# LayerNorm, 32-head attention and a mish gate on one core: b1 loaded as 14 rows, x tiles 1 and 3 on a second DMA queue, one tile's statistics on ScalarE, and a lead-in ordered by other planner numbers

## The chip, the cores and the metric

The kernel runs on one core of a Trainium2 chip. Its engines run programs of their own and wait for each other through semaphores: TensorE (PE, with its weight loads shown as PEld), VectorE (DVE), ScalarE (ACT), GpSimd (POOL) and SyncE (SP), which here does nothing but start DMA transfers. Other engines can start transfers too, on queues of their own.

The metric is the device time of one execution in microseconds. It is the median of several runs. One more execution was recorded by the hardware profiler; all durations below are from that one.

## The reference

All arrays are float32: x is 2048x512, wq and wo 512x512, wk and wv 512x16, w1 512x1792, b1 1792, w2 1792x512. The work is a LayerNorm without gain, attention with 32 query heads of width 16 over one shared key and value head, and a dense layer with mish whose result gates the attention's.

```python
xn = _layernorm(x, axis=-1)
# attention
q = (xn @ wq).reshape(B, S, 32, 16).transpose(0, 2, 1, 3)
k = xn @ wk
v = xn @ wv
p = softmax(einsum("bhqd,bkd->bhqk", q, k) * 16 ** -0.5)
o = einsum("bhqk,bkd->bhqd", p, v)
s = o.transpose(0, 2, 1, 3).reshape(B, S, 512) @ wo
# gate
h = xn @ w1 + b1
act = h * tanh(softplus(h))
g = silu(act @ w2)
return x + s * g
```

## The kernel before

**The tiling.** The 2048 rows of x are 16 tiles of 128 rows, in four chunks of four. To keep float32 precision on TensorE, a matrix is split into a high and a low part (type fp32r), and a product is three matmuls (high by high, high by low, low by high). So weights are loaded raw (`rawwq`, `rawws`, `rawwb`), the high part is copied by ACT (L467) and the low part subtracted on POOL (L169). There is one raw buffer of each kind, so that a load on SP's queue waits until POOL has split the one before it.

**The steady state.** Once the kernel is under way, each step of about 2.9 us on PE does, for the attention, scores twice: `m` (L1069) with the keys as columns, from which DVE takes row maxima (`mb`, L1073, 0.6 us each), and `e` (L1041), from which ACT makes the exponentials (`pts`, L1046); it sums the values (`pv`, L1127); and it fills PE's rest with matmuls of the dense layers (`xps`, L116). Those groups end in an eviction by ACT (`hb` with the bias `b1c`, L785), and mish runs as a chain of small jobs on ACT and POOL: Exp (`t`, L791), three operations on POOL (`t`, `u`, `u`), a product on POOL (`hb`), then Ln and Exp on ACT (`t`, L800 and L804), and another product on POOL.

**The lead-in.** The first 80 us have no such steps yet. There x is loaded and normalized, transposed on PE (`xp`, L298), multiplied with wq (`xps`, L112), wk and wv (`kp`, L339); the q rows go through small DMAs into the tiles `qt` (L741, twelve for each head, from `qh` and `ql`), and the key tile `ks` is written by ACT (high part, L344) and by DVE or POOL (low part), after which a DMA copies it to the other half of the partitions (`k_move`, L355; chunks 1 to 3 as two moves). As soon as q and a chunk of keys are there, the m matmuls of head 0 run, then those of head 1, each two halves: in the names, `m_0_24` is half 0 of block 24, whose keys are in chunk 3 (blocks 0 to 7 use chunk 0, and so on; blocks 4 to 7 of each eight use the later q DMAs). `qt_77` is head 0 and `qt_78` head 1. When head 0 has all 64 maxima, `c_rows` (L1092 to L1112) reduces them and sends them by eight DMAs into `qt_77`, after which the first wave of steps starts (first `xps` at L116).

**What sets the order.** The program is written by a list scheduler in Python. Each operation of the lead-in is a `task` on an engine with a planned duration, dependencies, an earliest time and a priority (L1302 to L1366); a loop takes what can start first, issues it, and advances that engine's planned time. Where PE has nothing ready, it emits three matmuls of a dense group (`fill(3)`) or a matmul without use that keeps PE's clock up (`keep_warm`, L1380, tile `warm`). The instructions of each engine then run on the chip in just this order, whatever the true durations are. So numbers in this planner move instructions on all engines. `xat` is the planned arrival time of an x tile; the tasks of the norm are `norm_a` (`ve`), `norm_b` (`rstd`, two ACT operations) and `norm_c` (DVE, first chunk) or `norm_d` (six small POOL operations, other chunks). The statistics of tiles 0 to 11 are `bn_stats` and `bn_aggr` on DVE (L239, L240), those of tiles 12 to 15 two accumulating passes on ACT (L244, L248).

**The bias.** `b1c` holds b1 as 128 rows by 14 columns, column t for hidden units 128 t to 128 t + 127. It is loaded by one DMA on SP's queue (L1288) that gathers single floats. Its only readers are the `hb` evictions (L785).

Of the kernel before, what the change touches and what calls it, by code (L numbers as in the profile page):

```python
# [14 lines left out]
F32 = mybir.dt.float32  # L15
F32R = mybir.dt.float32r
AF = mybir.ActivationFunctionType
# [3 lines left out]
P = 128  # L21
S = 2048
D = 512
# [7 lines left out]
NFT = F // P  # L31
# [91 lines left out]
def block_kernel(ctx: ExitStack, tc: tile.TileContext, x, wq, wk, wv, wo, w1, b1, w2, out):  # L123
    nc = tc.nc
    cp = ctx.enter_context(tc.tile_pool(name="const", bufs=1))
    sb = ctx.enter_context(tc.tile_pool(name="work", bufs=2))
    ps_e = ctx.enter_context(tc.tile_pool(name="ps_e", bufs=3, space=bass.MemoryType.PSUM))
    ps_m = ctx.enter_context(tc.tile_pool(name="ps_m", bufs=3, space=bass.MemoryType.PSUM))
    ps_v = ctx.enter_context(tc.tile_pool(name="ps_v", bufs=1, space=bass.MemoryType.PSUM))
# [4 lines left out]
    pe, act, dve, pool, sp = nc.tensor, nc.scalar, nc.vector, nc.gpsimd, nc.sync  # L134
# [51 lines left out]
    ident = cp.tile([P, P], F32, name="ident")  # L186
# [15 lines left out]
    b1c = cp.tile([P, NFT], F32, name="b1c")  # L202
# [4 lines left out]
    xr = x.rearrange("o (t p) d -> (o t) p d", p=P)  # L207
# [11 lines left out]
    xin = {}  # L219

    def load_x(c):
        for tt in range(4):
            if 4 * c + tt < NPT:
                xin[c, tt] = pts[:, 4 * c + tt]
            else:
                xin[c, tt] = sb.tile([P, D], F32, tag=("y0", "sc")[tt % 2], name=f"xin{c}_{tt}", bufs=1)
            sp.dma_start(xin[c, tt], xr[4 * c + tt])
            if (c, tt) == (1, 0):
                sp.dma_start(wkv[:, 0], wk.rearrange("(t p) n -> p t n", p=P))
                sp.dma_start(wkv[:, 1], wv.rearrange("(t p) n -> p t n", p=P))  # L230
                wk_split()

    mvs = cp.tile([P, NKT, 2], F32, name="mvs")

    nms = cp.tile([P, 4], F32, name="nms")

    def stats(t):
        st = sb.tile([P, 6], F32, tag="st", name=f"st{t}")
        dve.bn_stats(st, xin[divmod(t, 4)])  # L239
        dve.bn_aggr(mvs[:, t], st)  # L240

    def stats_sum(t):
        w = sb.tile([P, D], F32, tag="u", name=f"sq{t}", bufs=2)
# [80 lines left out]
    vp_of = {}  # L324
# [38 lines left out]

    def v_transpose(c):
        if c == 0:
            vp = vp_of[c] = ps_v.tile([P, 4, 32], F32, tag="v", name=f"vp{c}")
            for tt in range(4):
                pe.transpose(vp[:, tt], vt_of[c][0:32, P * tt:P * (tt + 1)], ident[0:32, 0:32])
        else:
            vp = vp_of[c] = ps_v.tile([P, 2, 2, HALF], F32, tag="v", name=f"vp{c}")  # L370
            for j in range(2):
                pe.transpose(vp[:, j], vt_of[c][:, P * j:P * (j + 1)], ident)

    def v_out(c):
        if c == 0:
            dve.tensor_copy(vaug[:, 0:4, 0:DH], vp_of[c][:, :, 16:32])
        else:
            act.activation(vaug[:, 4 * c:4 * c + 4, 0:DH].rearrange("p (h j) n -> p h j n", h=2),
                           vp_of[c][:, :, :, 48:64].rearrange("p j h n -> p h j n"), AF.Copy)
# [867 lines left out]
    def task(eng, us, fn, deps=(), **kw):  # L1247
        t = Task(eng, us, fn, deps, **kw)
        plan[eng].append(t)
        return t  # L1250
# [28 lines left out]

    step[0] = (0.0 - E0) / STEP_US  # L1280
    new_xt("w")
    xat = {0: 3.4, 1: 3.8, 2: 4.6, 3: 5.3}
    dma_t[0], T["SP"] = 6.4, 2.0
    load("wq")
    load_x(1)
    xat.update({t: landed(DMA_US) for t in range(4, 8)})
    load("ws")
    sp.dma_start(b1c, b1.rearrange("(t p) -> p t", p=P))  # L1288
    load_x(2)
    load_x(3)  # L1290
    xat.update({t: landed(DMA_US) for t in range(8, 16)})
# [11 lines left out]
        b.append([t, *users])  # L1303

    st = [task("DVE", 0.83, lambda t=t: stats(t), at=xat[t], prio=t // 4 * 2) for t in range(12)]
    for t in range(12, 16):
        ss = task("ACT", 0.8, lambda t=t: stats_sum(t), at=xat[t], prio=4)
        st.append(task("ACT", 0.8, lambda t=t: stats_var(t), [ss], prio=4))
    kv_done = None
    for c in range(NC):  # L1310
        z = slice(4 * c, 4 * c + 4)
        ne, eng = (("POOL", pool), ("DVE", dve))[c == 0]
        na = task(ne, 0.2, lambda z=z, eng=eng: norm_a(z, eng), st[z])
        nb = task("ACT", 0.45, lambda z=z: norm_b(z), [na], prio=c and 1)
        nrm = task(ne, 0.8 if c == 0 else 1.0, lambda z=z, n=(norm_d, norm_c)[c == 0]: n(z), [nb])
        xs = []
        for t in range(4 * c, 4 * c + 4):
            e, us = ("ACT", 0.8) if t % 2 or c == 3 else ("DVE", 0.55) if c == 0 else ("POOL", 0.8)
            sc = task(e, us, lambda t=t: x_scale(t), [nrm], prio=c and 1)
            tr = task("PE", 0.6, lambda t=t: x_transpose(t), [sc], fill=c > 0)  # L1320
            if c == 0:
                hi = task("ACT", 0.5, lambda t=t: x_high(t), [tr])
                lo = task("DVE", 0.62, lambda t=t: x_low(t), [hi], lat=-0.9 if t == 3 else 0.1)
            else:
                lo = task("ACT", 0.62, lambda t=t: x_copy(t), [tr], prio=1)
            if t != 3:
                bank("e", 3, tr, [lo])
            xs.append(lo)
        if c == 0:
            st[4].deps.append(nrm)  # L1330
            for k in st[5:12]:
                k.deps.append(xs[-1])

            def q_first():
                xt_done[0] = step[0]
                fill(12)
            xs = [task("PE", 2.8, q_first, xs)]
        else:
            for k in range(2):
                def keep_x(c=c, k=k):  # L1340
                    xt_keep(c, k)
                    landed(KEEP_US / 2)
                task("SP", 0.5, keep_x, xs, prio=2)
        kus = 0.5 if c else 0.7
        k0 = kp = task("PE", kus, lambda c=c: k_proj(c, (0,)), xs)
        for dt in range(1, 4):
            kp = task("PE", kus, lambda c=c, dt=dt: k_proj(c, (dt,)), [kp], lat=0.0)
        kv_done = kp
        kh = task("ACT", 0.76 if c else 0.59, lambda c=c: k_high(c), [kp])
        def low(c=c):  # L1350
            k_low(c)
            if c == 0:
                kready[0] = now[0] + 0.85, 1e9
        vc = task("ACT", 0.4 if c else 0.59, lambda c=c: v_copy(c), [kp])
        kl = task("POOL", 1.4, low, [kh, vc]) if 0 < c < 3 else task("DVE", 0.86 if c else 0.68, low, [kh])
        if c == 0:
            for t in plan["ACT"]:
                if t.prio == 4:
                    t.deps.append(kh)

        def mv(c=c):
            k_move(c)
            kready[c] = (kready[0][0] if c == 0 else now[0] + 3.1, now[0] + (3.1 if c else 2.6))
        moved = task("SP", 1.0 if c else 0.5, mv, [kl])
        if c == 0:
            lead["moved"] = moved  # L1366
        if c == 0:
            vc.deps = [kl]
        bank("v", 1, k0, [kh, vc] if 0 < c < 3 else [kl, vc])
        vtr = task("PE", 0.5, lambda c=c: v_transpose(c), [vc], fill=c > 0)  # L1370
        vo = task("ACT" if c else "DVE", 0.24, lambda c=c: v_out(c), [vtr])
        bank("v", 1, vtr, [vo])

# [302 lines left out]
```

## Time and profile before

| | |
|---|---|
| median of 3 runs | 1568.08 us (1567.94 to 1568.29) |
| the profiled execution | 1567.96 us |
| its span, first to last instruction | 1566.2 us |
| granted TensorE clock | 1.00 of full speed |
| PE busy | 1554.0 us, 99% of the span |
| DVE busy | 1348.7 us, 86% |
| ACT busy | 1290.5 us, 82% |
| POOL busy | 635.7 us, 41% |
| first m matmul of head 0 | 22.07 us after the span's start |
| first matmul of the first wave (L116) | 79.73 us |

Times in the views are microseconds from the start of the span, and the profiled execution is 1.8 us longer than its span. A row of the timeline gives start, duration, engine, line of the kernel, operation, output and inputs, shapes, and how many instructions are drawn together; in square brackets stands how long the engine was idle before it, and what ended that. "SPq" is SP's queue of DMA starts, whose rows are the time that SP took to start the transfer, not the transfer. "issue" is idle time that no release seen in the profile explains. A row of a chain of waits gives start, duration and what the end was waiting for then.

### The profile page before, as it was taken

The numbers are of one execution on the slowest core, as the hardware profiler recorded it, in microseconds if no ns is written. First come the engines' busy times: TensorE is split into PE (matmuls) and PEld (weight loads), VectorE is DVE, ScalarE is ACT, GpSimd is POOL, SyncE is SP. The second block draws the span as 40 slices with busy tenths as digits, with TensorE's granted clock in tenths as the row PEclk, the third lists the DMA queues.
The fourth block names the chain that finished last, engine by engine and source line by source line (L and its number), as shares of the span: only waits on it lengthen the run. The fifth ranks groups of instructions, "written<-read, shape, count | busy, mean of one in ns | idle before, by whom it ended". The sixth has DMA issues, their size and how long they took to land.

```text
span 1566.2 us, 31403 instructions
## 1 busy us (share of the span) xinstructions
PE 1554.0 (99%) x11723; PEld 873.7 (56%) x11723; DVE 1348.7 (86%) x2281; ACT 1290.5 (82%) x2501; POOL 635.7 (41%) x668
## 2 busy tenths in 40 slices
PE   9999999999999999999999999999999999999998
PEld 5555655655555565565555556556555555655644
DVE  7988888888988988888898988888889998888844
ACT  6488888789898778977989788897788978888796
POOL 5787449356356202431625422163152323314122
PEclk9999999999999999999999999999999999999999
DMA  7243134133151303203113320322321213031110
GB/s 220 75 138 119 46 100 150 29 112 112 42 160 50 108 16 112 72 20 104 52 56 112 92 92 17 104 67 76 105 59 41 97 56 111 24 99 32 34 63 28
DMA packets 73863, 125.47 MB, mean 80 GB/s; under 512 B 21536, under 2 KB 35136, under 8 KB 73712
## 3 DMA queue, kind: packets, MB, share of 16 engines
q1 hardware_dynamic: 73568, 123.21, 25.4%
q8 instruction: 93, 1.52, 0.4%
q14 instruction: 58, 0.48, 0.1%
q10 hardware_dynamic: 144, 0.26, 0.0%
HBM read 75.57 MB, written 26.21 MB: 65 GB/s over the span
## 4 chain that ended last, share of the span: by engine, by line
PE 96%; DVE 1%; ACT 1%; DMA 1%; issue 0%; POOL 0%; SPq 0%; POOLq 0%
PE xps L116 43%; PE pv L1127 32%; PE m L1069 12%; PE e L1041 7%; PE xps L112 1%; DVE mb L1073 1%; PE wop L116 1%; PE kp L339 0%; DMA pts<-in_dram 0%; DVE st L239 0%; DMA qt<-ql 0%; DMA rawwb<-in_dram 0%; ACT pts L1046 0%; PE y2ps L116 0%; PE wop L112 0%
## 5 line engine op out<-in xcount | busy, mean ns | idle before, releaser
L1073 DVE TENSOR_REDUCE mb<-m 128x1 f32<-128x512 f32 x2048 | 1266.7, 683 | 169.2 <-PE m L1069 136.0
L1046 ACT ACTIVATE pts<-e 128x512 f32<-128x512 f32 x2048 | 1066.2, 607 | 219.8 <-PE e L1041 153.9
L1069 PE MATMUL m<-ks,qt 48*128 48x512 f32 (+1 forms) x2048 | 842.5, 425 | 0.9 <-DVE mb L1073 0.5
L1041 PE MATMUL e<-qt,ks 64*128 64x512 f32 x2048 | 749.4, 407 | 0.4 <-ACT pts L1046 0.4
L1127 PE MATMUL pv<-pts,vaug 128*32 128x512 f32 x4096 | 532.8, 603 | 0.0
L1069 PEld LDWEIGHTS m<-ks,qt 48*128 48x128 f32 (+1 forms) x2048 | 367.8, 185 | 106.1 <-DVE mb L1073 52.4
L1041 PEld LDWEIGHTS e<-qt,ks 64*128 64x128 f32 x2048 | 372.8, 186 | 29.2 <-ACT pts L1046 23.2
L116 PE MATMUL xps<-wbs,act 64*128 64x512 f32 x1248 | 315.3, 397 | 0.0
L116 PE MATMUL xps<-xt,ws 64*128 64x512 f32 x1128 | 313.2, 410 | 0.4 <-ACT pts L1046 0.3
L116 PEld LDWEIGHTS xps<-xt,ws 64*128 64x128 f32 x1128 | 194.4, 185 | 183.3 <-ACT pts L1046 121.4
L116 PEld LDWEIGHTS xps<-wbs,act 64*128 64x128 f32 x1248 | 226.2, 185 | 65.7 <-ACT pts L1046 32.7
L1127 PEld LDWEIGHTS pv<-pts,vaug 128*32 128x32 f32 x4096 | 87.4, 108 | 150.6 <-issue 142.1
L169 POOL TENSOR_TENSOR hb<-hb,t 128x512 f32<-128x512 f32 x56 | 72.3, 1291 | 168.7 <-ACT t L804 88.4
L179 POOL TENSOR_SCALAR t<-t 128x512 f32<-128x512 f32 x56 | 34.4, 614 | 174.6 <-ACT t L791 174.4
L116 PE MATMUL xps<-xt,wq 64*128 64x512 f32 x336 | 93.0, 409 | 0.0
L116 PEld LDWEIGHTS xps<-xt,wq 64*128 64x128 f32 x336 | 57.9, 185 | 55.2 <-ACT pts L1046 37.7
L169 POOL TENSOR_TENSOR oc<-oc,sc 128x512 f32<-128x512 f32 (+1 forms) x16 | 20.6, 1287 | 153.1 <-DMA wbs<-w 39.8
L116 PE MATMUL xps<-wbs,ot_all 64*128 64x512 f32 x288 | 79.3, 407 | 0.0
L116 PEld LDWEIGHTS xps<-wbs,ot_all 64*128 64x128 f32 x288 | 49.5, 184 | 46.9 <-ACT pts L1046 28.5
L169 POOL TENSOR_TENSOR act<-hb,act 128x512 fp32r<-128x512 f32 x56 | 72.2, 1289 | 4.7
L169 POOL TENSOR_TENSOR hb<-hb,u 128x512 f32<-128x512 f32 x56 | 72.2, 1290 | 4.4
L169 POOL TENSOR_TENSOR u<-u,t 128x512 f32<-128x512 f32 x56 | 71.9, 1285 | 4.7
(151 smaller groups left out, 884.9 us busy)
## 6 DMA issues: line engine op xcount, KB each, us to landing
wbs<-w SPq DMA_DIRECT2D x38, 512.0 KB
ws<-w SPq DMA_DIRECT2D x36, 512.0 KB
qt<-qh SPq DMA_DIRECT2D x256, 32.0 KB
w<-wbs SPq DMA_DIRECT2D x14, 512.0 KB
wq<-wq SPq DMA_DIRECT2D x14, 512.0 KB
wbs<-wo SPq DMA_DIRECT2D x12, 512.0 KB
rawws<-in_dram SPq DMA_DIRECT2D x20, 256.0 KB
w<-ws SPq DMA_DIRECT2D x10, 512.0 KB
```

Of the source, the lines that this page charges most:

```text
L112: self.pe.matmul(ps, self.lhs(), self.rhs(), start=(self.k == 0), stop=(self.k == self.tot - 1))
L116: i = self.pe.matmul(ps, self.lhs()[o], self.rhs()[o], start=(self.k == 0 and self.halves == 0), stop=(self.k == self.tot - 1 and self.hal ...
L169: eng.tensor_tensor(out=o, in0=a, in1=b, op=op)
L179: pool.tensor_scalar(o, o, lim, 0.0, op0=ALU.min, op1=ALU.max)
L1041: pe.matmul(e, ks[o:o + 64, P * k:P * (k + 1)], q[o:o + 64, p], start=True, stop=True)
L1046: x = act.activation(dst, e, AF.Exp, scale=0.25)
L1069: pe.matmul(m, q[o, p, P * t:P * (t + 1)], ks[o, C * kb:C * (kb + 1)], start=True, stop=True)
L1073: return dve.reduce_max(out=mb_of[v][:, kb, z:z + 1], in_=m, axis=AX.X)
L1127: pe.matmul(o[32 * j:32 * j + 32], vaug[:, k], pt, start=(k == 0), stop=(k == 15))
```

## The change

It has four parts.

1. Tiles 1 and 3 of the first chunk of x are started by ACT on its own DMA queue; SP starts tiles 0 and 2, and all the rest as before.
2. b1 is loaded as 14 rows of 128 consecutive floats (`b1r`). PE transposes it into the same PSUM tile as the first chunk's values (`vp`), and ACT copies it from there into `b1c`. The DVE copy of the values into `vaug` reads the same tile and stands ahead of it.
3. The statistics of tile 1 are made on ACT by `stats_one`: two passes over the tile and two copies of single columns.
4. Three planner numbers: the arrivals of x tiles 0 and 1, the duration of `norm_d`, and that of the new statistics task.

```diff
@@ load_x
-            sp.dma_start(xin[c, tt], xr[4 * c + tt])
+            (act if c == 0 and tt % 2 else sp).dma_start(xin[c, tt], xr[4 * c + tt])
...
+    b1r = cp.tile([NFT, P], F32, name="b1r")
...
+    ms1 = cp.tile([P, 2], F32, name="ms1")
+
+    def stats_one():
+        x_ = xin[0, 1]
+        w = [sb.tile([P, D], F32, tag=g, name=f"s1{g}", bufs=2) for g in "ut"]
+        act.activation(w[0], x_, AF.Identity, scale=-1.0 / 8192, accum_out=ms1[:, 0:1])
+        act.activation(w[1], x_, AF.Square, scale=1.0 / 16, bias=ms1[:, 0:1], accum_out=ms1[:, 1:2])
+        act.activation(mvs[:, 1, 0:1], ms1[:, 0:1], AF.Copy, scale=-16.0)
+        act.activation(mvs[:, 1, 1:2], ms1[:, 1:2], AF.Copy, scale=0.5)
...
@@ v_transpose, c == 0
-            vp = vp_of[c] = ps_v.tile([P, 4, 32], F32, tag="v", name=f"vp{c}")
+            v_b1 = ps_v.tile([P, P + NFT], F32, tag="v", name=f"vp{c}")
+            vp = vp_of[c] = v_b1[:, 0:P].rearrange("p (t n) -> p t n", n=32)
+            vp_of["b1"] = v_b1[:, P:P + NFT]
+            pe.transpose(vp_of["b1"], b1r, ident[0:NFT, 0:NFT])
...
@@ v_out, c == 0
             dve.tensor_copy(vaug[:, 0:4, 0:DH], vp_of[c][:, :, 16:32])
+            act.activation(b1c, vp_of["b1"], AF.Copy)
...
-    xat = {0: 3.4, 1: 3.8, 2: 4.6, 3: 5.3}
+    xat = {0: 4.3, 1: 4.3, 2: 4.6, 3: 5.3}
...
-    sp.dma_start(b1c, b1.rearrange("(t p) -> p t", p=P))
+    sp.dma_start(b1r, b1.rearrange("(t p) -> t p", p=P))
...
+    plan["DVE"].remove(st[1])
+    st[1] = task("ACT", 2.2, stats_one, at=xat[1])
...
-        nrm = task(ne, 0.8 if c == 0 else 1.0, lambda z=z, n=(norm_d, norm_c)[c == 0]: n(z), [nb])
+        nrm = task(ne, 0.8 if c == 0 else 1.8, lambda z=z, n=(norm_d, norm_c)[c == 0]: n(z), [nb])
```

The planner then writes the lead-in in another order on every engine. From the first matmul of the first wave on, PE's program is the same as before. PE's `warm` matmuls at L1380 go from 14 to 5. Line numbers of the changed kernel are larger by 11 to 15 behind the new functions (L1069 becomes L1084). The three places that the prediction speaks of follow.

The first place is PE between the projection of k and v of chunk 0 (`kp`) and the first m matmuls. Before:

```order
L339 MATMUL kp_268<-xt_173,wk_90 64x512 x12
L1380 MATMUL warm<-qt_79 128x512
L298 MATMUL xp_312<-ident,pts 128x128 x4
L1380 MATMUL warm<-qt_79 128x512
L298 MATMUL xp_323<-ident,pts 128x128 x4
L1380 MATMUL warm<-qt_79 128x512
L298 MATMUL xp_334<-ident,pts 128x128 x4
L1069 MATMUL m_0_0_343<-ks,qt_77 128x512
```

Now:

```order
L350 MATMUL kp_273<-xt_175,wk_90 64x512 x12
L112 MATMUL xps<-xt_175,xtw 128x512 x6
L309 MATMUL xp_326<-ident,pts 128x128 x4
L1084 MATMUL m_0_0_335<-ks,qt_77 128x512
L1084 MATMUL m_0_1_340<-ks,qt_77 128x512
L1084 MATMUL m_0_2_350<-ks,qt_77 128x512
L380 MATMUL vp_353<-ident,b1r 128x14
L382 MATMUL vp_353<-ident,vt_338 128x32 x4
```

The three warm matmuls are gone, six matmuls of a dense group (`xps` from the first w1 tile `xtw`) stand ahead of the first transposes of chunk 1, and only one x tile of that chunk is transposed ahead of the first m.

On ACT at the same place, the new copy of the bias stands among the norm's operations. Now (there was no such row before):

```order
L355 ACTIVATE ks<-kp_273 48x512
L211 ACTIVATE pts<-pts,nbias,rstd 128x512 x2
L371 ACTIVATE vt_338<-kp_273 32x512
L327 ACTIVATE xf_0_346<-xp_326 128x2x128
L327 ACTIVATE xf_1_347<-xp_326 128x2x128
L272 ACTIVATE rstd<-ve 128x4
L273 ACTIVATE rstd<-rstd 128x4
L391 ACTIVATE b1c<-vp_353 128x14
L255 ACTIVATE sq_366,nms<-pts 128x512
```

The high part of the keys (`ks`) now comes ahead of both x tiles' scaling instead of between them. `b1c` must follow the DVE copy `vaug`, which on DVE stands behind the first four maxima.

The second place is SP's queue around the move of key chunk 3 (the last `ks<-ks`, two transfers). Before:

```order
L355 DMA ks<-ks 48x256 x2
L514 DMA rawws_654<-in_dram 128x4x128
L516 DMA rawwb_675<-in_dram 128x512
L966 DMA xtk_677<-xf_0_616 128x1024
L966 DMA xtk_677<-xf_1_617 128x1024
L514 DMA rawws_701<-in_dram 128x4x128
L516 DMA rawwb_715<-in_dram 128x512
L355 DMA ks<-ks 48x256 x2
L514 DMA rawws_809<-in_dram 128x4x128
L514 DMA rawws_887<-in_dram 128x4x128
```

Now:

```order
L366 DMA ks<-ks 48x256 x2
L529 DMA rawws_674<-in_dram 128x4x128
L531 DMA rawwb_695<-in_dram 128x512
L981 DMA xtk_699<-xf_0_636 128x1024
L981 DMA xtk_699<-xf_1_637 128x1024
L529 DMA rawws_762<-in_dram 128x4x128
L531 DMA rawwb_774<-in_dram 128x512
L366 DMA ks<-ks 48x256 x2
L529 DMA rawws_882<-in_dram 128x4x128
L1127 DMA qt_77<-cr_912 2x8x32 x8
```

The rows read alike, but the loads ahead of the last move are the next pair of weights: one pair more has been loaded further up. A load waits for POOL's split of the tile before it (`xtw` and `wbs`), and these splits now stand behind the first mish chain. On POOL, before:

```order
L169 TENSOR_TENSOR xtw<-rawws_654,xtw 128x512
L169 TENSOR_TENSOR wbs<-rawwb_675,wbs 128x512
L179 TENSOR_SCALAR t_0_738<-t_0_738 128x512
L794 TENSOR_SCALAR u_0_739<-t_0_738 128x512
L169 TENSOR_TENSOR u_0_739<-u_0_739,t_0_738 128x512
L169 TENSOR_TENSOR hb_0_730<-hb_0_730,u_0_739 128x512
L169 TENSOR_TENSOR xtw<-rawws_701,xtw 128x512
```

and now:

```order
L169 TENSOR_TENSOR xtw<-rawws_583,xtw 128x512
L169 TENSOR_TENSOR wbs<-rawwb_598,wbs 128x512
L179 TENSOR_SCALAR t_0_704<-t_0_704 128x512
L809 TENSOR_SCALAR u_0_705<-t_0_704 128x512
L169 TENSOR_TENSOR u_0_705<-u_0_705,t_0_704 128x512
L169 TENSOR_TENSOR hb_0_697<-hb_0_697,u_0_705 128x512
L169 TENSOR_TENSOR xtw<-rawws_674,xtw 128x512
L169 TENSOR_TENSOR wbs<-rawwb_695,wbs 128x512
```

So the load `rawwb_774`, and behind it the key move, wait for the split of `rawwb_695`, four mish operations later than the split of `rawwb_675` that they waited for.

The third place is the start of the first wave. PE before, from the last group ahead of it:

```order
L1069 MATMUL m_1_9_969<-ks,qt_78 128x512
L112 MATMUL xps<-xt_173,ws_844 128x512 x6
L1069 MATMUL m_0_10_983<-ks,qt_78 128x512
L1069 MATMUL m_1_10_986<-ks,qt_78 128x512
L1069 MATMUL m_0_11_991<-ks,qt_78 128x512
L1069 MATMUL m_1_11_994<-ks,qt_78 128x512
L116 MATMUL xps<-xt_173,ws_913 128x512
L1069 MATMUL m_1_12_999<-ks,qt_78 128x512
```

and now:

```order
L1084 MATMUL m_1_9_967<-ks,qt_78 128x512
L112 MATMUL xps<-xt_175,ws_833 128x512 x6
L1084 MATMUL m_0_10_983<-ks,qt_78 128x512
L1084 MATMUL m_1_10_986<-ks,qt_78 128x512
L1084 MATMUL m_0_11_989<-ks,qt_78 128x512
L1084 MATMUL m_1_11_992<-ks,qt_78 128x512
L112 MATMUL xps<-xt_175,ws_833 128x512 x3
L116 MATMUL xps<-xt_175,ws_921 128x512
L1084 MATMUL m_1_12_1007<-ks,qt_78 128x512
```

The last three matmuls of the dense group now stand behind the four m matmuls, so that nothing lies between that group's end and the wave that wants its PSUM bank.

On ACT at this place, before:

```order
L800 ACTIVATE t_1_796<-u_1_797,two 128x512
L785 ACTIVATE hb_4_981<-xps,b1c 128x512
L1046 ACTIVATE pts<-e_0_0_1_1003 128x512
L1046 ACTIVATE pts<-e_0_1_1_1011 128x512
L1046 ACTIVATE pts<-e_1_0_1_1019 128x512
L1046 ACTIVATE pts<-e_1_1_1_1025 128x512
L804 ACTIVATE t_1_796<-t_1_796 128x512
L1046 ACTIVATE pts<-e_0_0_0_1045 128x512
L1046 ACTIVATE pts<-e_0_1_0_1053 128x512
L1046 ACTIVATE pts<-e_1_0_0_1061 128x512
L1046 ACTIVATE pts<-e_1_1_0_1067 128x512
L800 ACTIVATE t_2_919<-u_2_920,two 128x512
```

and now:

```order
L815 ACTIVATE t_1_801<-u_1_802,two 128x512
L819 ACTIVATE t_1_801<-t_1_801 128x512
L815 ACTIVATE t_2_895<-u_2_896,two 128x512
L819 ACTIVATE t_2_895<-t_2_895 128x512
L800 ACTIVATE hb_4_1003<-xps,b1c 128x512
L1061 ACTIVATE pts<-e_0_0_1_1011 128x512
L1061 ACTIVATE pts<-e_0_1_1_1019 128x512
L1061 ACTIVATE pts<-e_1_0_1_1027 128x512
L1061 ACTIVATE pts<-e_1_1_1_1033 128x512
L1061 ACTIVATE pts<-e_0_0_0_1052 128x512
L1061 ACTIVATE pts<-e_0_1_0_1060 128x512
L1061 ACTIVATE pts<-e_1_0_0_1068 128x512
```

Three mish operations (`t_1` at L804, `t_2` at L800 and L804, the latter just behind the last row shown of before) have moved from between the first exponentials to ahead of them.

## The prediction

> **What bounds the kernel now.** I read the page first: busy time by engine, and the chain of work that ended last.
>
> ```profile
> PE 1554.0 (99%) x11723; PEld 873.7 (56%) x11723; DVE 1348.7 (86%) x2281; ACT 1290.5 (82%) x2501; POOL 635.7 (41%) x668
> PE 96%; DVE 1%; ACT 1%; DMA 1%; issue 0%; POOL 0%; SPq 0%; POOLq 0%
> ```
>
> PE is the bound nearly everywhere, and behind the lead-in its program does not change. So the change can only move the time at which PE settles into its steady pace, and every microsecond of that goes one for one into the end. Next I asked for busy time by stretch around the first wave, for the sums over DVE in the lead-in, and for the longest pieces of the chain of waits.
>
> ```profile
> 70.00:80.00 10.00, 9.43 (x42) 5.65 (x44) 9.60 (x19) 3.95 (x7) 7.91 (x8) 1.00 0.19 53
> 80.00:90.00 10.00, 8.77 (x54) 4.55 (x54) 9.21 (x16) 8.45 (x16) 5.30 (x6) 1.00 0.40 145
> 90.00:100.00 10.00, 10.00 (x84) 5.51 (x83) 8.78 (x15) 8.47 (x18) 9.42 (x11) 1.00 0.54 176
> ...
> L1073 DVE TENSOR_REDUCE mb<-m 128x1 f32<-128x512 f32 x85 | 52.2, 682 | 5.4 <-PE m L1069 5.2
> ...
> 1.65 4.33 DMA pts<-in_dram
> 48.50 3.53 DMA rawwb<-in_dram
> 74.71 7.93 DVE mb L1073 x13
> ```
>
> The columns of the first three rows are busy time (and instructions) of PE, PEld, DVE, ACT and POOL, then the clock. From 90 us PE is full; between 80 and 90 it is not, and the chain runs through 13 of DVE's maxima there. Ahead of that, DVE makes 85 maxima by 80 us and idled 5.4 us in front of them. So there are two things to win: an earlier start of the wave (79.73 us), and a wave that isn't held by DVE and ACT.
>
> **Edits at the very start: about nothing.**
>
> ```profile
> 3.48 0.69 DVE L239 BATCH_NORM_STATS2 st<-pts 128x6 f32<-128x512 f32 x1 [1.53 <-DMA pts<-in_dram]
> 4.30 0.66 DVE L239 BATCH_NORM_STATS2 st<-pts 128x6 f32<-128x512 f32 x1
> 5.99 0.69 DVE L239 BATCH_NORM_STATS2 st<-pts 128x6 f32<-128x512 f32 x1 [0.81 <-DMA pts<-in_dram]
> 7.73 0.17 DVE L258 TENSOR_SCALAR ve<-mvs 128x4 f32<-128x4 f32 x1
> 7.94 0.20 ACT L261 ACTIVATE rstd<-ve 128x4 f32<-128x4 f32 x1 [5.92 <-DVE ve L258]
> ```
>
> DVE waited for tile 2 until 5.98 us (1.65 + 4.33 in the chain); the statistics of tiles 2 and 3 follow without a further wait, and `ve` comes at 7.73, so they take 0.87 us each. Taking tile 1's off DVE frees time in which DVE waits anyway; on ACT its four operations lie in the 5.92 us that ACT is idle before `rstd`. What counts is when the later of tiles 2 and 3 lands, since both still need DVE. Tile 1 is in by 4.30; tile 0 was in by 3.48, so tiles come 0.82 apart or closer. At the best two more are there 0.55 apart behind 4.30, at 5.4, and `ve` comes at 5.4 + 2 x 0.87 = 7.1; if both land only when tile 3's statistics start now, at 5.99 + 0.87 = 6.86, it is 8.6. I take 7.8, nearest to the row of tile 2: 0.0, with ends of -0.6 and +0.9.
>
> [...]
>
> **First m, from 22.07 to about 21.4.**
>
> ```profile
> 8.53 5.10 SPq L227 DMA_DIRECT2D pts<-in_dram  x6
> 18.67 0.40 PE L1380 MATMUL warm<-qt 128*128 128x512 f32 x1
> 18.84 0.81 ACT L211 ACTIVATE pts<-pts,nbias,rstd 128x512 f32<-128x512 f32 x1 [1.79 <-POOL nbias L282]
> 19.56 0.58 ACT L344 ACTIVATE ks<-kp 48x512 fp32r<-48x512 f32 x1
> 20.24 0.68 DVE L169 TENSOR_TENSOR ks<-kp,ks 16x512 fp32r<-16x512 f32 x1 [0.17 <-ACT ks L344]
> 22.07 0.94 PE L1069 MATMUL m<-ks,qt 64*128 64x512 f32 x3 [0.33 <-DMA qt<-ql]
> ```
>
> Six x tiles behind b1's load took 5.10 us to start; without its single-float pieces the queue runs ahead, so the q rows, whose landing ended the wait at 22.07, land no later, perhaps earlier. `ks` now goes ahead of the x scaling on ACT: it can start near 18.85, 0.7 us earlier, and be complete near 20.3. PE does six dense matmuls (1.67 us, a row of the next fence) and one x tile (four transposes, an estimate of 0.7 by the same row) from 18.8: 21.2. So the first m comes at 21.2 to 22.07; I take 21.4, -0.7.
>
> **The key move of chunk 3 swallows that and costs 1.0.** The second place of the change: SP's move waits behind a load, and that for POOL.
>
> ```profile
> 47.73 0.96 PE L112 MATMUL xps<-xt,xtw 128*128 128x512 f32 x3
> 52.76 1.29 POOL L169 TENSOR_TENSOR wbs<-rawwb,wbs 128x512 fp32r<-128x512 f32 x1 [0.63 <-ACT wbs L467]
> 53.65 0.68 ACT L785 ACTIVATE hb<-xps,b1c 128x512 f32<-128x512 f32 x1
> 54.08 0.33 SPq L516 DMA_DIRECT2D rawwb<-in_dram  x1
> 54.38 1.67 PE L112 MATMUL xps<-xt,xtw 128*128 128x512 f32 x6 [0.24 <-ACT hb L785]
> 55.08 0.61 POOL L179 TENSOR_SCALAR t<-t 128x512 f32<-128x512 f32 x1 [1.03 <-ACT t L791]
> 55.13 1.16 SPq L355 DMA_DIRECT2D ks<-ks  x2
> 57.84 1.28 POOL L169 TENSOR_TENSOR hb<-hb,u 128x512 f32<-128x512 f32 x1
> 60.20 0.74 PE L1069 MATMUL m<-ks,qt 64*128 64x512 f32 x4
> ```
>
> Before, the load at 54.08 waited for the split that ended at 54.05, and the key move went out at 55.13; the first m of chunk 3 (`m_0_24`) ran at 60.20. Now the first `hb` group ends some six dense matmuls earlier, where the group of 47.73 to 48.69 stood. Its eviction (0.68) then starts at 48.7, or up to 1.0 later if ACT is late (below); POOL's chain starts 1.43 behind the eviction's start (53.65 to 55.08): 50.1 to 51.1. It takes 4.04 (55.08 to 59.12), the two splits 1.29 each: 56.7 to 57.7. The load goes out (0.33), then the moves: 57.1 to 58.1. A load of 256 KB took 3.53 to land in the chain; the moves are smaller, and I take 2.9 for both with ends of 2.2 and 3.5: `m_0_24` at 59.3 to 61.6, middle 61.2 since I hold ACT late for the likelier: +1.0 (-0.9 to +1.4).
>
> ACT is late by the new bias copy. It stands behind DVE's `vaug`, that behind four maxima: the first m at 21.4, 0.5 for it, 4 x 0.61, and 0.2 for the copy, 24.5, while ACT has the work ahead of it done 1 to 1.7 us sooner. All that is queued on ACT behind it (statistics, x copies, the split of wq, and by POOL's split SP's next weight load with q transfers behind it) shifts by as much, less what ACT idles later.
>
> **From there to the wave: 1.3 less.** Behind `m_0_24` PE's program has four m and three dense matmuls fewer (28 m for 32, 42 dense for 45), since these have been done ahead of it.
>
> ```profile
> 62.47 0.74 PE L1069 MATMUL m<-ks,qt 64*128 64x512 f32 x4
> 64.79 0.97 PE L112 MATMUL xps<-xt,xtw 128*128 128x512 f32 x3 [0.69 <-ACT qf L727]
> 70.35 0.97 PE L112 MATMUL xps<-xt,xtw 128*128 128x512 f32 x3 [0.78 <-ACT hb L785]
> 79.73 0.50 PE L116 MATMUL xps<-xt,ws 64*128 64x512 f32 x1
> ```
>
> Four m take 0.74 and three dense 0.96: -1.7. The eviction ahead of the wave was hidden by four m (the row at 79.73 shows no idle time ahead of it); with three matmuls moved behind them it is bare, as at 70.35: +0.8. The wait for `qf` at 64.79 (0.69) gets four m to hide it: -0.4. Sum -1.3, ends -2.1 (the eviction hidden after all) and -0.9 (`qf` not hidden). So the wave starts at 79.73 + 1.0 - 1.3 = 79.4.
>
> **The dropped warm matmuls: nothing of their own.**
>
> Nine go, at most 0.40 us each by the one at 18.67, so up to 3.6 us of PE. The order has them all far ahead of `m_0_24`, so this too ends in its wait; what of it is real shows in the rival below in which that wait doesn't bind. The one new transpose of `b1r` lies in the same stretch and is costed at nothing for the same reason; were the cover gone, it would cost no more than a warm matmul, 0.4.
>
> **The first three steps: 2.0 less.**
>
> ```profile
> 83.75 0.62 ACT L804 ACTIVATE t<-t 128x512 f32<-128x512 f32 x1
> 85.90 0.18 PEld L116 LDWEIGHTS xps<-xt,ws 64*128 64x128 f32 x1 [0.64 <-ACT pts L1046]
> 86.22 0.72 ACT L800 ACTIVATE t<-u,two 128x512 f32<-128x512 f32 x1
> 86.98 0.63 ACT L804 ACTIVATE t<-t 128x512 f32<-128x512 f32 x1
> 88.14 0.18 PEld L1041 LDWEIGHTS e<-qt,ks 64*128 64x128 f32 x1 [0.49 <-ACT pts L1046]
> 89.56 0.18 PEld L116 LDWEIGHTS xps<-xt,ws 64*128 64x128 f32 x1 [0.84 <-ACT pts L1046]
> ```
>
> Three mish operations stood between exponentials, 0.62 + 0.72 + 0.63 = 1.97 us, and PE waited for ACT 0.64 + 0.49 + 0.84 = 1.97 us in the same stretch. They now lie ahead of the wave, where ACT was busy 3.95 of 10 us. DVE, the other brake (the 13 maxima from 74.71 in the chain, 0.61 each), enters the wave with less behind it: the three matmuls and the bare eviction give it 0.96 + 0.8 us more ahead of the wave, nearly three maxima. It made 16 in the stretch from 80 to 90 in 9.21 us; 13 take 7.5. I take -2.0, with ends of 0 (DVE stays the brake) and -2.5 (all that DVE allows).
>
> **Sum.** Against the profiled execution's own 1567.96 us (span 1566.2; 0.12 below the median, which I neglect): start and first m -0.7, swallowed; +1.0 at the key move, -1.3 to the wave, -2.0 in the first steps: -2.3, 1565.7.
>
> **Rivals.**
> *The key move doesn't bind.* If the moves land as early as 59.3, `m_0_24` comes 0.9 sooner than before instead of 1.0 later: -0.9 - 1.3 - 2.0 = -4.2, 1563.8. For it: every step of POOL's chain is short, and PE has up to 3.6 us less to do ahead. Against: ACT's new wait. DVE bounds it: it idles 5.2 us for m in all by 80 us, so no more than that can be won.
>
> *The first steps stay held by DVE.* Then the 2.0 fall away and -0.3 is left: 1567.7. For it: DVE ran from 74.7 on without idling; against: fewer m wait at its door.
>
> *Slower: POOL's split holds SP's queue longer.* Each us by which the split of `rawwb` ends behind 57.7 delays the key move, `m_0_24` and the wave by one. With the shift on ACT at its full 1.7 us, plus tiles landing late (+0.8), 2.5 beyond the middle: 1568.2; it is slower than now from 2.3 us beyond the middle, and at 5 us beyond it gives 1570.7.
>
> *The clock.* Fewer warm matmuls leave longer gaps on PE. The only slow matmuls of this trace are the first:
>
> ```profile
> 1.99 7.24 PE L1295 MATMUL warm<-qt 128*128 128x512 f32 x24 [1.99 <-DVE one L191]
> ```
>
> These 24 took 7.24 us; at 0.24 each (six dense in 1.67, three in 0.96) they would take 5.8. One more such start costs 1.5: 1567.2. Against it: the clock stands at 1.00 in the three stretches above, and six dense matmuls take the place of the first warm ones. [...]
>
> *The edits don't do what they say.* Tiles on two queues land no earlier; that is in the bounds of the start and changes little, since its gain is swallowed anyway.
>
> **Chances.** 0.2% of this kernel is 3.1 us, about what a measurement can tell. My forecast (-1 to -3.1) 0.58; the key move doesn't bind 0.23; DVE stays the brake or the clock falls 0.12; slower than before 0.07, of which about 0.05 beyond 3.1 us. Faster by over 0.2% is the second with a little of the first: 0.25; slower 0.05; same 0.70. The range reaches from the rival of 1563.8 to just above no change: 1563.5 to 1568.3.
>
> **What would show it.** Right: `ve` near 7.8, the first m near 21.4, ACT idle before the b1c copy, the key move of chunk 3 behind its load near 58, `m_0_24` near 61, the wave at 79.4, only exponentials on ACT in its first two steps, and the first three steps 2 us shorter. I'd be wrong if `m_0_24` runs before 60 (more gain), or if PE waits for `mb` past the second step as before (no gain).

## The result

The changed kernel runs 1565.51 us in the median of 13 executions, before 1570.39 us in the median of 13 in the same comparison. The ratio is 0.9978, with a 95% interval of 0.9972 to 0.9985: 2.3 to 4.4 us faster, 3.4 us in the middle. The medians themselves differ by more, 4.9 us, and the profiled executions by less, 1566.29 against 1567.96 us. That these figures don't agree has a cause, which the experiments found: TensorE's mean granted clock is below 0.999 in some executions of both kernels, and not equally often (in 5 of 24 of the changed kernel over two sets, in 38 of 92 of before). In the two profiles of the changed kernel the granted clock falls to 0.50 in the lead-in, for 3.42 and 10.24 us. Before was run again in each of the three comparisons below, 92 times in all. Each run gives, beside the median, how many executions had a mean granted clock of 0.999 or more (called "at the full clock" here), and their median. This sorts out the long falls only: a fall of 3.4 us at half speed takes 1.7 us of 1564.5, 0.0011, off the mean, and the profiled execution after, which had one, still reads 0.999. The three profiles below 0.999 show falls of 6.8 to 13.7 us, and every execution below 0.999 is counted as one with a long fall. Two executions with a mean clock far below the others (0.654 and 0.949) are left out.

The lines of the profile after that answer to the prediction's, from the timeline (the last two rows are the first `e` of the first and of the fourth step):

```profile
1.99 8.55 PE L1310 MATMUL warm<-qt 128*128 128x512 f32 x24 [1.99 <-DVE one L191]
4.56 0.69 DVE L240 BATCH_NORM_STATS2 st<-pts 128x6 f32<-128x512 f32 x1 [2.62 <-DMA pts<-in_dram]
5.70 0.69 DVE L240 BATCH_NORM_STATS2 st<-pts 128x6 f32<-128x512 f32 x1 [0.22 <-DMA pts<-in_dram]
7.52 0.17 DVE L269 TENSOR_SCALAR ve<-mvs 128x4 f32<-128x4 f32 x1
21.39 0.97 PE L1084 MATMUL m<-ks,qt 64*128 64x512 f32 x3
24.64 0.18 ACT L391 ACTIVATE b1c<-vp 128x14 f32<-128x14 f32 x1 [1.44 <-DVE vaug L390]
56.99 1.30 POOL L169 TENSOR_TENSOR wbs<-rawwb,wbs 128x512 fp32r<-128x512 f32 x1
58.31 0.33 SPq L531 DMA_DIRECT2D rawwb<-in_dram  x1
58.74 1.15 SPq L366 DMA_DIRECT2D ks<-ks  x2
62.07 0.83 PE L1084 MATMUL m<-ks,qt 64*128 64x512 f32 x4 [1.28 <-DVE mb L1088]
80.10 0.49 PE L116 MATMUL xps<-xt,ws 64*128 64x512 f32 x1 [0.78 <-ACT hb L800]
80.45 0.39 PE L1056 MATMUL e<-qt,ks 64*128 64x512 f32 x1
88.41 0.39 PE L1056 MATMUL e<-qt,ks 64*128 64x512 f32 x1
```

Most of the path is there as forecast: the first m at 21.39, ACT idle 1.44 us before the bias copy, the key move of chunk 3 held by POOL's split and SP's load until 58.74, the eviction ahead of the wave bare (0.78 us idle). The move and the first m of chunk 3 (62.07) come later than the ends given for them, though. This profile puts the wait at 62.07 down to a maximum on DVE that ended at 62.01; in the run with four extra matmuls below the same m started at 61.66, while that maximum ran to 61.75, and waited for the move. So here too it is probably the move. The wave starts 0.4 us later than before and is then shorter: from the first `e` to the fourth step 7.96 us. Before, these were 9.83 us:

```profile
80.08 0.39 PE L1041 MATMUL e<-qt,ks 64*128 64x512 f32 x1
89.91 0.39 PE L1041 MATMUL e<-qt,ks 64*128 64x512 f32 x1
```

What the prediction did not have is in the clock. Busy time of PE (and matmuls) in stretches of one microsecond of the profile after, then the granted clock, where it was not 1.00:

```profile
25.00:26.00 1.00, 1.00 (x5) 0.54 0.27 66
26.00:27.00 1.00, 1.00 (x3) 0.50 0.26 55
27.00:28.00 1.00, 1.00 (x7) 0.50 0.15 37
28.00:29.00 1.00, 1.00 (x5) 0.75 0.14 33
```

TensorE's granted clock was 0.50 from 25.08 to 28.50 us (the 0.54 and the 0.75 give the parts of the first and last microsecond), in the stretch from which the warm matmuls were taken. In the profile before, no microsecond of the first 90 is below 1.00.

### The profile page after: what moved, and what is told of

It reads as the page before. It is cut to its first block, busy times and chain, and to the rows that moved or that the text cites. A ratio compares the mean times of both kernels' runs of the same rounds, so it can differ in the third digit from the quotient of the medians.

```text
span 1564.5 us, 31399 instructions
## 1 busy us (share of the span) xinstructions
PE 1553.6 (99%) x11715; PEld 877.1 (56%) x11715; DVE 1347.6 (86%) x2279; ACT 1292.8 (83%) x2509; POOL 635.1 (41%) x667
## 4 chain that ended last, share of the span: by engine, by line
PE 97%; DVE 2%; ACT 1%; POOL 0%; issue 0%; DVEq 0%
PE xps L116 43%; PE pv L1142 32%; PE m L1084 12%; PE e L1056 7%; DVE mb L1088 1%; PE xps L112 1%; PE warm L1310 1%; PE kp L350 0%; PE xp L309 0%; PE wop L116 0%; ACT pts L1061 0%; DVE e L888 0%; PE y2ps L116 0%; PE wop L112 0%; ACT hb L800 0%; ACT xt L318 0%
## 5 line engine op out<-in xcount | busy, mean ns | idle before, releaser
L1084 PE MATMUL m<-ks,qt 48*128 48x512 f32 (+1 forms) x2048 | 844.1, 425 | 1.3 <-DVE mb L1088 1.3
L1084 PEld LDWEIGHTS m<-ks,qt 48*128 48x128 f32 (+1 forms) x2048 | 369.9, 185 | 105.8 <-DVE mb L1088 50.8
```

The lines of the kernel that those rows point to most:

```text
L1084: pe.matmul(m, q[o, p, P * t:P * (t + 1)], ks[o, C * kb:C * (kb + 1)], start=True, stop=True)
```

## The experiments

Theory "order": the gain comes from the new order, above all from the first steps of the wave, and the loads, the bias and the statistics only matter through it. Rival "edits": these save the time. After the first four runs a third was added, "clock".

**The changed kernel again.** No edit.

> The changed kernel again, beside the others on one chip. Both theories: 3.0 to 3.5 us faster than before (ratio 0.9978). Its trace tells how much the start of the clock varies: if the 24 first warm matmuls take 7.2 us as in the profile before, rather than the 8.55 of the profile after, the first m should come near 20.7 instead of 21.39, and the span should be about a microsecond shorter than 1564.5.

1564.98 us in the median of 11 (ratio 0.9981, 0.9973 to 0.9990). The 24 first matmuls took 8.28 us, so the trace does not show the early start. It shows a longer fall of the clock instead:

```profile
24.00:25.00 1.00, 0.99 (x4) 0.73 0.26 64
25.00:26.00 1.00, 1.00 (x5) 0.50 0.17 43
...
33.00:34.00 1.00, 1.00 (x8) 0.50 0.61 174
34.00:35.00 1.00, 1.00 (x6) 0.65 0.13 31
```

That execution took 1568.05 us, and its wave started at 81.96 instead of 80.10. Over both sets of the changed kernel (24 executions), 19 had a clock of 0.999 or more, median 1565.12; the five others 1568.27. Of the 19, twelve read 1.000 (median 1564.97) and seven 0.999 (1565.60), among them the profile after with its one fall. So five of 24 is the count of long falls; how many had a short one isn't known.

**One planner number alone.**

```diff
-        nrm = task(ne, 0.8 if c == 0 else 1.0, ...
+        nrm = task(ne, 0.8 if c == 0 else 1.8, ...
```

> The kernel before with one planner number changed: the duration of norm_d 1.8 instead of 1.0. By the order it gets the changed kernel's order on all engines, without the ACT queue, the b1 rows and the ACT statistics. Theory 'order' (the gain comes from the new order): at least three quarters of the gain, 1565.0 to 1566.0 where before has 1568, and the first three steps of the wave about 2 us shorter than before. Theory 'edits' (the gain comes from the loads and the statistics): less than a quarter of it, above 1567.2.

1569.09 us in the median of 11 (ratio 1.0003, 0.9994 to 1.0012): neither theory's number. But one execution had the full clock, the profiled one, and took 1564.29; the ten others had clocks between 0.995 and 0.997, and took 1567.1 to 1570.7. In the profiled one PE waited for q ahead of the first m, and the first three steps took 7.98 us (78.96 to 86.94):

```profile
21.76 0.92 PE L1069 MATMUL m<-ks,qt 64*128 64x512 f32 x3 [1.44 <-DMA qt<-ql]
78.62 0.50 PE L116 MATMUL xps<-xt,ws 64*128 64x512 f32 x1 [0.78 <-ACT hb L785]
```

So the order alone gives the short wave, and loses the clock nearly always. Its time without a fall rests on that one execution.

**All edits, with that number back.**

```diff
-        nrm = task(ne, 0.8 if c == 0 else 1.8, ...
+        nrm = task(ne, 0.8 if c == 0 else 1.0, ...
```

> The changed kernel with the duration of norm_d back at 1.0: all edits of loads, bias and statistics stay, and the order is like the one before, with three mish operations on ACT among the first exponentials. Theory 'order': within 0.8 us of before, 1567.2 to 1568.5. Theory 'edits': within 0.8 us of the changed kernel, 1564.5 to 1566.

1567.94 us (ratio 0.9995, 0.9986 to 1.0004), nine of 11 at the full clock with 1567.78, where before had 1567.72 in the same comparison. The first three steps took 9.83 us again (80.61 to 90.44). The edits without the order give nothing, as "order" had it.

**b1 as single floats again, same order.**

```diff
-    sp.dma_start(b1r, b1.rearrange("(t p) -> t p", p=P))
+    sp.dma_start(b1c, b1.rearrange("(t p) -> p t", p=P))
...
-            pe.transpose(vp_of["b1"], b1r, ident[0:NFT, 0:NFT])
-            act.activation(b1c, vp_of["b1"], AF.Copy)
```

> The changed kernel with b1 loaded as single floats again, without its transpose and without the ACT copy; the order is otherwise the same. Theory 'order': the bias copy's wait on ACT (1.44 us) is gone and SP is 2.3 us later with six x loads; neither is on the path for long: within 0.7 us of the changed kernel. Theory 'edits': at least 1.5 us slower than the changed kernel, since q lands later.

1568.28 us in the median of 12 (ratio 0.9991, 0.9982 to 1.0000). Four at the full clock had 1564.93, as the changed kernel; eight did not, with 1568.93. By the median that is 3.3 us more than the changed kernel in the same comparison, the size that "edits" asked for, but it comes with the clock. In its profile PE waited for q ahead of the first m, and behind it the clock was at half for 13.7 us:

```profile
21.62 0.93 PE L1081 MATMUL m<-ks,qt 64*128 64x512 f32 x3 [0.99 <-DMA qt<-ql]
...
23.00:24.00 1.00, 1.00 (x4) 0.59 0.26 62
...
36.00:37.00 1.00, 1.00 (x6) 0.58 0.33 92
```

So the bias by rows costs and saves nothing at the full clock, as far as four executions show it, and with it long falls are rarer: 5 of 24 executions, 8 of 12 without. The traces show what it does for q: with single floats the six x loads behind b1 took 5.12 us to start (2.73 in the profile after), the DMA engines were still busy for 0.66 of the stretch from 18.00 to 21.40 us, and PE, which waited for the q transfer started at 18.05, began 3.57 us behind that start, at 21.62. In the profile after the share is 0.19, and the same transfer, started at 18.76, was in by 21.39, in 2.63 us at most. Whether PE's idle time ahead of the first m brings the fall is not shown: the profile of the order alone had 1.44 us of it and kept the clock.

**The clock, from both sides.** One matmul without use ahead of the transposes of tiles 5 to 8 of the changed kernel, into the PSUM bank that the transposes then fill; then two; and the kernel before without its warm matmuls behind 18 us. The order is otherwise unchanged.

```diff
         xp_of[t] = ps.tile([P, NDT, P], F32, tag=tag, name=f"xp{t}")
+        if t in (5, 6, 7, 8):
+            for _ in range(1):
+                pe.matmul(xp_of[t].rearrange("p a b -> p (a b)"), qts[2][:, 0, 0:P], qts[2][:, 0], start=True, stop=True)
```

> The changed kernel with one matmul without use ahead of the transposes of each of the x tiles 5 to 8 (four in all, in the stretch from 21 to 29 us, where the order before had warm matmuls and the changed one has none). Theory 'clock' (most of the spread, and the part of the gain that is missing, comes from the granted clock falling to half at 23 to 25 us): fewer executions below a clock of 0.999, median 1564.3 to 1565. Theory 'no clock' (the drop is chance, of the chip and not of the order): the same share of executions with a low clock, and the four matmuls cost up to 4 x 0.34 = 1.4 us, 1565 to 1567.

> The same with two such matmuls ahead of each of the four tiles. Theory 'clock': all executions at a clock of 0.999 or more, median 1564 to 1565, the first wave near 79 us. Theory 'no clock': up to 2.7 us slower than the changed kernel with the same clocks.

```diff
 def keep_warm():
...
+        if now[0] < 18.0:
             pe.matmul(w, qts[2][:, 0, 0:P], qts[2][:, 0], start=True, stop=True)
```

> The kernel before without its nine warm matmuls behind 18 us, in the same order otherwise. Theory 'clock': the clock falls in most executions, 0.998 and less, and it is 1 to 4 us slower than before. Theory 'no clock': PE has 3.1 us less to do in the lead-in, clocks as before, 0 to 2 us faster.

With one: 1565.45 us, all 8 executions at 0.999 or more (ratio 0.9976, 0.9967 to 0.9986). With two: 1565.54, all 11. Before without its nine: 1570.14, nine of 11 below 0.999 (ratio 1.0001, 0.9992 to 1.0010). The last one's profile:

```profile
26.00:27.00 1.00, 1.00 (x4) 0.56 0.16 35
...
32.00:33.00 1.00, 1.00 (x4) 0.53 0.75 191
```

So "clock" holds for the falls, on one side more firmly than on the other. None of the 45 executions of the changed kernel with extra matmuls (here and in three variants below) had a long fall, against five of 24 without; eight alone would not settle it. Leaving nine out of before brings a long fall in nine of 11, against 15 of 32 of before in the same comparison, and there chance isn't excluded. "Clock" does not hold for the times: with the extra matmuls they lie above its 1564 to 1565, in the range of "no clock", and before without its nine is no slower by the ratio, where 1 to 4 us were expected.

Before at the full clock took 1567.72 us in the first comparison, 1568.08 in the second and 1567.51 in the third, so times of different comparisons are set against it: the changed kernel is 2.8 us below it (1564.91 in the first), with four extra matmuls 2.6, with eight 2.5. The extra matmuls cost 0.2 to 0.3 us.

**Two mish operations back among the exponentials.** In the planner, ACT's free time is no longer given to mish behind 74 us, which moves `t_2`'s two operations (and, by a place each, later ones).

```diff
-                if not plan["POOL"]:
+                if not plan["POOL"] and s < 74.0:
                     act_jobs(1)
```

> The changed kernel with two of the three mish operations (t_2 at L815 and L819, 0.72 + 0.63 us) put back behind the first exponentials. If what they took from ACT between exponentials is what held PE, the time from the first e to the fourth step goes from 7.96 to 9.3 us, and the kernel is 1.0 to 1.4 us slower at the same clock. If DVE's backlog held PE instead, less than 0.4 us.

From the first `e` to the fourth step:

```profile
80.00 0.39 PE L1056 MATMUL e<-qt,ks 64*128 64x512 f32 x1
88.64 0.39 PE L1056 MATMUL e<-qt,ks 64*128 64x512 f32 x1
```

8.64 us, 0.68 more than 7.96, where 1.35 us of work came back: half. At the full clock it took 1565.54 (seven executions, the profiled one with a fall of 3.4 us among them), 2.5 below before and so 0.3 slower than the changed kernel. By the trace it lies between the two expectations, by the time in the second, though 0.3 us is little against the spread: mish on ACT is part of what held the wave. That the rest is DVE's smaller backlog is the reading left over, and no run took that apart.

**The key move off SP's queue.** On top of the kernel with four extra warm matmuls.

```diff
-            sp.dma_start(f(ks[HALF - o:HALF - o + 48, t]), f(ks[o:o + 48, t]))
+            (act if c == 3 else sp).dma_start(f(ks[HALF - o:HALF - o + 48, t]), f(ks[o:o + 48, t]))
```

> The kernel of the run with one extra warm matmul per tile, and the key move of chunk 3 started by ACT on its queue instead of by SP behind the two weight loads. If the move's wait behind POOL's splits is what holds the lead-in (PE idled 1.10 us for it at 61.66), it goes out near 57.0 instead of 58.4, the wait at the first m of chunk 3 is gone, and the wave starts 0.5 to 1.1 us earlier: 1564.4 to 1565.0. If DVE's chain of maxima is the bound instead, less than 0.3 us.

1563.83 us, all eight at the full clock (ratio 0.9975, 0.9964 to 0.9985). That is 3.7 below before at the full clock in its comparison, where the kernel without it was 2.6 below: a gain of 1.1 us. First the rows with the move on SP, then with it on ACT:

```profile
58.57 1.15 SPq L369 DMA_DIRECT2D ks<-ks  x2
61.66 0.69 PE L1087 MATMUL m<-ks,qt 64*128 64x512 f32 x3 [1.10 <-DMA ks<-ks]
79.70 0.50 PE L116 MATMUL xps<-xt,ws 64*128 64x512 f32 x1 [0.78 <-ACT hb L803]
```

```profile
55.23 1.23 ACTq L369 DMA_DIRECT2D ks<-ks  x2
59.26 0.73 PE L1087 MATMUL m<-ks,qt 64*128 64x512 f32 x4
77.39 0.50 PE L116 MATMUL xps<-xt,ws 64*128 64x512 f32 x1 [0.78 <-ACT hb L803]
```

The wait is gone, and the move went out at 55.23, earlier than the 57.0 expected. The wave is 2.3 us earlier, of which 1.0 was there at the first m already (20.46 against 21.42, since the 24 first matmuls took 7.62 instead of 8.58 us); 1.35 came behind it, against 0.5 to 1.1 expected. So the key move did bind.

**Fewer first matmuls.** `NWARM = 20` instead of 24, on top of that.

> The kernel of the run with the key move on ACT's queue, with 20 first warm matmuls instead of 24. In executions in which the clock rises late (24 take 8.0 to 8.6 us) PE reaches the first transposes before the normalized x does, 0.5 to 0.9 us earlier; where it rises early nothing changes. Median 0.3 to 0.7 us below the run with 24. If fewer first matmuls cost the clock, some executions fall below 0.999 and are 1 to 3 us slower.

1563.81 us, all seven at the full clock: no gain and no loss. In its profile the 20 took 7.21 us, and PE's weight loads waited 0.53 us for the normalized x behind them.

**All x tiles on one queue,** with the four extra matmuls.

```diff
-            (act if c == 0 and tt % 2 else sp).dma_start(xin[c, tt], xr[4 * c + tt])
+            sp.dma_start(xin[c, tt], xr[4 * c + tt])
```

> The kernel of the run with one extra warm matmul per tile, with all x tiles on SP's queue again. If the second queue only saves time in issuing, the last of tiles 2 and 3 lands as in the profile before or up to 0.3 us later, and the time is the same within 0.3 us. If it brings the x tiles earlier, 0.3 to 1 us slower.

1565.00 us, eleven at the full clock, 2.5 below before; with two queues 2.6. So the second queue gains nothing in time. What it does is seen on DVE, whose statistics of tiles 0, 2 and 3 and `ve` with one queue were:

```profile
3.47 0.69 DVE L240 BATCH_NORM_STATS2 st<-pts 128x6 f32<-128x512 f32 x1 [1.52 <-DMA pts<-in_dram]
6.16 0.69 DVE L240 BATCH_NORM_STATS2 st<-pts 128x6 f32<-128x512 f32 x1 [1.79 <-DMA pts<-in_dram]
6.99 0.66 DVE L240 BATCH_NORM_STATS2 st<-pts 128x6 f32<-128x512 f32 x1
7.98 0.17 DVE L269 TENSOR_SCALAR ve<-mvs 128x4 f32<-128x4 f32 x1
```

With two queues tile 0 came 1.1 us later and tile 2 0.5 earlier (4.56 and 5.70), `ve` at 7.52, 0.5 earlier than with one.

**The order alone, with the clock kept up.** The kernel before with `norm_d` at 1.8, four matmuls without use ahead of the first m and two ahead of tiles 5 to 8.

> The kernel before with the duration of norm_d at 1.8, so with the order of the changed kernel and none of its other edits, and with warm matmuls: four ahead of the first m and two ahead of each of tiles 5 to 8. Theory 'order, if the clock holds': clock of 0.999 or more in most executions, and 1564.3 to 1565.5, as fast as with the other edits. Theory 'the edits are needed too': the clock holds, but 1566 or more.

1566.62 us, all 11 at the full clock (ratio 0.9986, 0.9978 to 0.9995): the clock holds, against ten long falls in 11 of the order alone. It is only 0.9 us below before at the full clock, where the changed kernel with four extra matmuls is 2.6 below, so "the edits are needed too" is what was met. Its first m waited for q until 22.79:

```profile
22.79 0.92 PE L1075 MATMUL m<-ks,qt 64*128 64x512 f32 x3 [1.35 <-DMA qt<-ql]
```

The same order without the extra matmuls took 1564.29 in its one execution at the full clock, with the first m at 21.76. From that profile to this one the wave comes 2.9 us later (81.52 against 78.62): 1.0 at the first m, where q landed later, and 1.9 behind it, where PE's chain holds eight of the extra matmuls. So both seem to have a part, on one pair of profiles. What the edits are worth once the clock is safe stays open, since no run has this order with only as many extra matmuls as it needs.

The executions at a glance (in us; "below before" is the distance to before at the full clock in the same comparison, for the changed kernel from its second set):

| kernel | executions | at 0.999 or more | their median | below before | the others' median |
|---|---|---|---|---|---|
| before | 92 | 54 | 1567.86 | | 1570.70 |
| changed | 24 | 19 | 1565.12 | 2.8 | 1568.27 |
| order alone | 11 | 1 | 1564.29 | 3.4 | 1569.11 |
| edits alone | 11 | 9 | 1567.78 | -0.1 | 1568.71 |
| changed, b1 as single floats | 12 | 4 | 1564.93 | 2.8 | 1568.93 |
| changed, 4 extra matmuls | 8 | 8 | 1565.45 | 2.6 | |
| changed, 8 extra matmuls | 11 | 11 | 1565.54 | 2.5 | |
| before without 9 warm ones | 11 | 2 | 1567.77 | 0.3 | 1570.23 |
| changed, two mish operations back | 10 | 7 | 1565.54 | 2.5 | 1568.92 |
| 4 extra, key move on ACT | 8 | 8 | 1563.83 | 3.7 | |
| 4 extra, key move on ACT, 20 first matmuls | 7 | 7 | 1563.81 | 3.7 | |
| 4 extra, x tiles on one queue | 11 | 11 | 1565.00 | 2.5 | |
| order alone, 12 extra matmuls | 11 | 11 | 1566.62 | 0.9 | |

## Why the prediction came out right, and where it was wrong

The forecast was 1565.7 (1563.5 to 1568.3), 2.3 us faster; measured were 1565.51, and 3.4 us by the ratio. At the full clock it is 2.7 to 2.8. Part of the agreement is chance: the sum starts from a profile of before without a fall and has no term for falls, which take 0.7 us on average from the changed kernel (below), and against that its gain at the full clock is 0.4 to 0.5 more than forecast. In the profile after, the path lands 0.7 us later at the wave than the 79.4 forecast, and its execution (1566.29) 0.6 above the forecast.

- **The very start, 0.0.** `ve` came at 7.52 for 7.8 forecast, inside the ends. With two queues tile 0 came 1.1 us later than with one, and the whole brought no time, though `ve` came 0.5 earlier. Missed was that PE need not be free by then: its first matmuls ran to 10.5 us.
- **First m, 21.4.** 21.39 was measured, with luck: the first matmuls took 8.55 us there for 7.24 before, so PE started its work 1.3 us later than the sum assumed; in a profile with an earlier start the first m was at 20.46, below the ends.
- **The key move, +1.0.** The mechanism was right: the move waits behind POOL's split and SP's load, and 1.1 us were gained when it was taken off SP. The size was too small: the move went out at 58.74 for 57.1 to 58.1, and the first m of chunk 3 came at 62.07 for 61.2, +1.9 and above the upper end of 61.6; without a fall, in the profile with four extra matmuls, it came at 61.66, +1.5. Wrong was "swallows": the move isn't fixed in time but shifts with the start. With the first m at 20.91 instead of 21.42 (eight extra matmuls against four) the first m of chunk 3, which waited for the move, came at 61.32 instead of 61.66 and the wave at 79.37 instead of 79.70, so two thirds of an earlier start were passed on in this one pair.
- **From there to the wave, -1.3.** From 62.07 to 80.10 it took 18.0 us, before 19.5: -1.5, inside the ends.
- **The first three steps, -2.0.** 7.96 for 9.83, -1.87: the size was right. The reason was half right: two of the three mish operations, 1.35 us, put back among the exponentials, cost 0.68.
- **The dropped warm matmuls, "nothing of their own".** This step failed. Long falls of the clock came in five of 24 executions of the changed kernel, at 3.15 us each, and in none of 45 with four or eight matmuls without use put back. Before without its nine had them in nine of 11, though its time was not clear of before's. So they do have a price, through the rival that I held unlikely.
- **The clock rival.** I put it aside since the clock stood at 1.00 in three stretches of one profile and six dense matmuls took the place of the first warm ones. They did, and in the profile after the granted clock fell to 0.50 all the same, with PE busy for 3.40 of the 3.42 us ahead of it; 5 of 24 executions of the changed kernel and 38 of 92 of before had long falls, at about 3 us each for the 1.5 put on the rival. The missing term is that share: 0.21 x 3.15 = 0.7 us on average for the changed kernel and 0.41 x 2.84 = 1.2 for before. That would be a further 0.5 us in favour of the change, but the two shares are not far enough apart to exclude chance. One profile of before without a fall had hidden it.
- **The other rivals.** "The key move doesn't bind" fell (PE waited 1.10 us for it). "The first steps stay held by DVE" fell. "Slower" fell.

## What to carry to other kernels

Where a reordering takes matmuls without use out of a lead-in, read the granted clock of every execution, not of one profile: here the new order alone was 3.4 us faster in the one execution that kept the clock and no faster in the median, and four matmuls without use, which cost about 0.2 us at the full clock, kept the changed kernel and three variants of it free of long falls in all 34 executions. Set times against the kernel before in the same comparison: at the full clock it differed by up to 0.6 us between comparisons, half of what the key move gained. And a DMA queued behind loads that wait for another engine's work can be worth a queue of its own: moving two small key transfers gave 1.1 us, and that version (1563.83 us) beats both kernels.

## What the runs showed of the hardware

The granted clock fell to 0.50 in the lead-in of five profiles, for different lengths. From the parts of the first and last microsecond, as above: 25.08 to 28.50 in the changed kernel is 3.42 us; 24.46 to 34.70 in its second profile 10.24; 23.18 to 36.84 with b1 as single floats 13.66; 26.12 to 32.94 in before without warm matmuls 6.82; and 25.00 to 28.42 with two mish operations back 3.42. What sets these lengths was not measured. In the 3.42 us ahead of the fall in the changed kernel's profile PE was busy for 3.40 (columns as in the prediction's first stretches: PE, PEld, DVE, ACT, POOL, then the clock):

```profile
21.66:25.08 3.42, 3.40 (x18) 1.89 (x18) 3.15 (x7) 1.92 (x7) 1.21 (x7) 1.00 0.28 70
25.08:28.49 3.41, 3.41 (x14) 2.31 (x13) 1.95 (x4) 3.38 (x10) 1.51 (x2) 0.50 0.19 45
```

What decides is not seen in such rows. The kernel with four extra matmuls, which kept the clock, issued just as many matmuls in the same stretch, and the kernel before, which kept it too in its profile, fewer and with more idle time. First four extra, then before:

```profile
21.66:25.08 3.42, 3.42 (x18) 2.09 (x18) 3.13 (x6) 1.92 (x7) 1.19 (x6) 1.00 0.28 70
21.66:25.08 3.42, 2.99 (x15) 1.80 (x14) 2.51 (x5) 3.26 (x11) 0.99 (x5) 1.00 0.31 74
```

So the granted clock fell behind a stretch with 3.40 us of PE busy, and stayed at 1.00 behind one with 2.99; what it goes by was not measured. The start varies as well: the same 24 first matmuls took from 7.20 to 8.58 us in these profiles; in those of before and after a single one of them took from 387 to 792 ns, 391 in the median before and 628 after. The granted clock reads 1.00 there in every profile, so that it rises early or late, as two of the expectations have it, was my reading and is not shown.
